# 64x64 TensorE tiles, half-partition loads on two queues and an early half-width start in a gated-attention + bilinear-FFN kernel

## The chip, the cores and the metric

One core of a Trainium2 chip runs the whole program. The metric is the device time of one execution in microseconds (us), less is better. Engines: TensorE (PE; PEld is its weight load), VectorE (DVE), ScalarE (ACT), GpSimd (POOL), and SyncE (SP), which only issues DMAs.

## The reference, cut to what matters

```python
# q, k, v, alpha: (B=4, H=8, S=768, D=48); per batch and head
state = alpha[t][:, None] * state + outer(k[t], v[t])
y[t]  = q[t] @ state
# x = y as (3072, 384); weights 384x1536, 384x1536, 1536x384
out = ((x @ w_a) * (x @ w_b)) @ w_out
```

## The kernel before

The sequence is cut into six chunks of 128 positions, and a chunk holds all four batches. The 64 partitions of a half g hold 64 position pairs of two batches; the position within a pair is the index r, a free index. The batch within a half is u.

For a chunk the attention runs through these stages: `load` (alpha, v, k, q; each tile in two DMAs of 64 partitions with rows of 384 bytes), `logs` (Ln on ACT, pair sums), `stA` (cumulative sums by a float32 matmul, then four Exp on ACT), `mul` (scaled Q and K, on POOL after the first chunk), `vcast` and `vshift` (V to bf16, then four DMAs move it to natural position order, `vb`), `decay`, `stC` (eight transposes, copied out as `qk`), `stD` (scores, times the causal mask, `m`), `stY` (output from the state `Sb` and from `vb`, copied to `xT`), `fill` (six small DMAs that complete `xT`: heads have 48 rows and lie in 64), and `stK` (state update).

The FFN of a chunk is 12 pairs `ff_a(f)`, `ff_b(f)` of three matmuls of 512 columns, and 4 `ff_o(m)` of 12 matmuls of 384 columns. The FFN of chunk c and the attention of chunks c+1 and c+2 are interleaved by hand: the tables `PLAN` and `STEADY` give the slot behind which each stage is written, a slot being one f (0 to 11) or one m (12 to 15). Every engine takes its instructions in the written order.

PSUM: tag `f` has four banks for the FFN (and for the first chunk's stages), `t1` and `t2` one each for `stC` and for `stA`/`stY`, `s2` two for `stD`/`stK`. At the start SP issues all loads of chunk 0 one after the other; POOL then issues 16 loads of w_a and w_b with a cast to bf16, three of w_out, and two memsets by which chunk 1's alpha and k loads are held back until then.

Of the kernel before, what the change touches and what calls it, by code (L numbers as in the profile page):

```python
# [11 lines left out]
ALU = mybir.AluOpType  # L12


@with_exitstack
def kernel(
# [14 lines left out]
    C = 128  # L31
# [50 lines left out]
    vz = cst.tile([C, B, KT, 2, DP], BF16, name="vz")  # L82
    nc.vector.memset(vz, 0.0)
# [24 lines left out]
    chunks = [Chunk(c) for c in range(NCH)]  # L108

# [4 lines left out]
    def load(ch, what, us):  # L114
# [53 lines left out]
    def decay(ch):  # L168
# [7 lines left out]
        for r in range(2):  # L176
            nc.sync.dma_start(out=ch.bl[r * DP:r * DP + D].rearrange("d b a -> d (b a)"),
                              in_=row[:, :, r, :].rearrange("g a d -> d (g a)"), allow_slow_non_contiguous=True)

    def stC(ch, u, h, tag="t1", act=False):  # L180
        i = ch.c % 2
        t = bank(tag, 4 if tag == "f" else 1, BF16, [C, 2, 2, 2, 2, HC])
        for p in range(2):
            for j, src in enumerate((Qp[i], Kp[i])):
# [5 lines left out]
        if act:  # L190
# [4 lines left out]
    def stD(ch, u, h, tags=None):  # L195
        qk = ch.qk[u, h]
        ch.m[u, h] = m = wk.tile([C, 2, 4, C], BF16, name="m", bufs=4)
        if tags is None:
            s2 = bank("s2", 1, F32, [C, 2, 4, C])
            sc = [s2[:, 0], s2[:, 1]]  # L200
        else:
            sc = [bank(t, 1, F32, [C, 4, C]) for t in tags]
        for p in range(2):
            for g in range(2):
                for r in range(2):
                    rs = slice(r * DP, (r + 1) * DP)
                    nc.tensor.matmul(sc[r][:, 2 * p + g, :], lhsT=qk[rs, 1, p, g, :], rhs=qk[rs, 0, p, g, :], start=True, stop=True)  # L207
        if tags is None:
            nc.vector.tensor_mul(m.rearrange("p r a s -> p (r a) s"), s2.rearrange("p r a s -> p (r a) s"), maskn(8))  # L209
        else:  # L210
            for r in range(2):
                nc.vector.tensor_mul(m[:, r], sc[r], maskn(4))

    def alloc_x(ch):

        ch.xT = wk.tile([128, KT + 1, B, C], BF16, name="xT")

    def evac(ch, u, ts, y, act=True, gaps=True):

        n = ts.stop - ts.start  # L220
        o_ = ch.xT[:, ts, u::2, :].rearrange("p t g (s r) -> p (t g) r s", r=2)
        i_ = y[:, :2 * n].rearrange("p a (r s) -> p a r s", r=2)
        for r in range(1 if gaps else 2):
            rs = slice(0, C) if gaps else slice(r * DP, r * DP + D)
            if act and r == 0:
                nc.scalar.activation(out=o_[rs], in_=i_[rs], func=AF.Copy)  # L226
            else:
                nc.vector.tensor_copy(o_[rs], i_[rs])  # L228

    def stY(ch, u, h):  # L230
        if not hasattr(ch, "xT"):
            alloc_x(ch)
        y = bank("t2", 1, F32, [C, 4, C])

        for p in range(2):
            for g in range(2):
                nc.tensor.matmul(y[:, 2 * p + g, :], lhsT=Sb[:, 2 * g + u, 2 * h + p, :], rhs=ch.qk[u, h][:, 0, p, g, :],  # L237
                                 start=(p == 0 and g == 0), stop=False, skip_group_check=True)
        for p in range(2):
            for g in range(2):  # L240
                for r in range(2):
                    hd = 2 * (2 * h + p) + r
                    nc.tensor.matmul(y[r * DP:r * DP + D, 2 * p + g, :], lhsT=ch.vb[:, 2 * g + u, hd * D:(hd + 1) * D], rhs=ch.m[u, h][:, r, 2 * p + g, :],  # L243
                                     start=False, stop=True, skip_group_check=True)
        evac(ch, u, slice(2 * h, 2 * h + 2), y, gaps=(ch.c > 1 or h == 1))

    def stYz(ch, u, tags, act):

        if u == 0:
            alloc_x(ch)  # L250
        for h, n in ((1, 1), (0, 2)):
            y = bank(tags, 4, F32, [C, 4, C])
            for p in range(n):
                for g in range(2):
                    for r in range(2):
                        nc.tensor.matmul(y[r * DP:(r + 1) * DP, 2 * p + g, :], lhsT=vz[:, 2 * g + u, 2 * h + p, r, :], rhs=ch.m[u, 1][:, r, 2 + g, :],
                                         start=(p == 0 and g == 0), stop=False, skip_group_check=True)
            for p in range(n):
                for g in range(2):
                    for r in range(2):  # L260
                        hd = 2 * (2 * h + p) + r
                        nc.tensor.matmul(y[r * DP:r * DP + D, 2 * p + g, :], lhsT=ch.vb[:, 2 * g + u, hd * D:(hd + 1) * D], rhs=ch.m[u, h][:, r, 2 * p + g, :],
                                         start=False, stop=True, skip_group_check=True)
            evac(ch, u, slice(2 * h, 2 * h + n), y, act=(h == 0))

    def fill(ch):
        for t in range(KT):
            for r in range(2):
                eng = nc.sync if ch.c > 1 else (nc.gpsimd, nc.scalar)[r]
                eng.dma_start(out=ch.xT[r * DP + D:(r + 1) * DP, t], in_=ch.xT[r * DP + t * G:r * DP + (t + 1) * G, KT])  # L270

    def stK(ch, u):
# [4 lines left out]
        for p in range(P2):  # L277
            for r in range(2):
                for g in range(2):
                    gs = slice(g * HC, (g + 1) * HC)  # L280
                    nc.tensor.matmul(kv[:, g, p * 2 * D:(p + 1) * 2 * D], lhsT=Kp[i][gs, u, r, 2 * p:2 * p + 2, :].rearrange("s h d -> s (h d)"),  # L281
                                     rhs=ch.vx[gs, r, u, 2 * p:2 * p + 2, :].rearrange("s h d -> s (h d)"), start=(r == 0), stop=(r == 1))
        tmp = None if ch.c == 0 else wk.tile([C, 2, P2, D], F32, name="tmp")
        for r in range(2):
            rs = slice(r * DP, r * DP + D)
            x = kv[rs, :, :P2 * 2 * D].rearrange("p g (a e) -> p g a e", a=P2)[:, :, :, r * D:(r + 1) * D]
            so = Sb[rs, u::2, :, r * DP:r * DP + D]
            bl = ch.bl[rs, u::2, :].rearrange("p g (a o) -> p g a o", o=1).broadcast_to([D, 2, P2, D])
# [183 lines left out]
```

## Time and profile before

| | |
|---|---|
| median of 3 runs | 245.22 us (244.45 to 245.22) |
| the profiled execution | 244.67 us |
| its span, first to last instruction | 242.8 us |
| PE busy | 202.2 us, 83% of the span |
| granted PE clock, mean | 0.93 |
| DMA | 30.31 MB, mean 125 GB/s |

A busy PE is an average over stages with different limits; the rows below cut the span by chunks. 1.9 us of the profiled execution lie outside the span.

### The profile page before, as it was taken

The page shows a single profiled execution, that of the slowest core. Times are in us where ns is not written, and L with a number is a line of the kernel's source. Part 1 is how long each engine was busy: PE and PEld are TensorE (multiplying, and loading weights), DVE is VectorE, ACT ScalarE, POOL GpSimd, SP SyncE. Part 2 cuts the span into 40 slices and gives each one's busy share as a digit, 9 for nine tenths or more (in the row PEclk, how much of TensorE's full clock was granted, in tenths as well). Part 3 has the DMA queues.
Part 4 walks back from the last instruction along what each step waited for, and adds up shares of the span by engine and source line. Part 5 has one row for each costly group of instructions (what it writes and reads, how often), then busy time and mean ns, then how long its engine had stood idle before and what let it go on. Part 6 is the DMA issues. An engine that isn't in the chain of part 4 may idle for free.

```text
span 242.8 us, 4155 instructions
## 1 busy us (share of the span) xinstructions
PE 202.2 (83%) x1556; PEld 109.9 (45%) x1576; DVE 126.4 (52%) x180; ACT 121.6 (50%) x194; POOL 73.0 (30%) x79
## 2 busy tenths in 40 slices
PE   0426699399862978998999999999998999999994
PEld 0124544135641333565455554555454555554452
DVE  3266737055234456862577932978625886215510
ACT  2545223574732674484654386544758445334421
POOL 3028610046020549032680235902238400000000
PEclk9985579859996599999999999999999999999999
DMA  7999999993996802999239992239992300120002
GB/s 125 190 205 201 162 179 204 215 208 73 160 173 132 203 19 51 176 204 221 68 69 180 191 153 80 68 71 197 191 146 100 97 3 0 49 99 3 0 32 97
DMA packets 67915, 30.31 MB, mean 125 GB/s; under 512 B 59716, under 2 KB 67128, under 8 KB 67896
## 3 DMA queue, kind: packets, MB, share of 16 engines
q1 hardware_dynamic: 64328, 26.42, 61.8%
q0 software_dynamic: 3472, 3.59, 9.7%
q8 instruction: 12, 0.20, 0.4%
q10 hardware_dynamic: 96, 0.05, 0.1%
q14 instruction: 7, 0.06, 0.1%
HBM read 25.98 MB, written 4.75 MB: 127 GB/s over the span
## 4 chain that ended last, share of the span: by engine, by line
PE 59%; DMA 14%; ACT 6%; issue 6%; POOL 6%; SPq 4%; DVE 2%; POOLq 0%; ACTq 0%; DVEq 0%
PE f L304 16%; PE f L311 16%; PE f L317 14%; DMA a_t<-in_alpha_dram 7%; SPq L118 4%; PE t L187 4%; PE s L207 3%; POOL Qp L166 3%; DMA k_t<-in_k_dram 3%; PE t L243 3%; DMA wa_t<-in_moe_w_a_dram 2%; PE t L158 2%; ACT la L137 2%; PE s L281 2%; PE t L237 2%
## 5 line engine op out<-in xcount | busy, mean ns | idle before, releaser
L304 PE MATMUL f<-xT,wa_t 128*128 128x512 bf16 x214 | 61.5, 395 | 7.1 <-ACT as__495 L306 3.9
L311 PE MATMUL f<-xT,wb_t 128*128 128x512 bf16 x198 | 58.6, 392 | 1.4 <-issue 0.6
L317 PE MATMUL f<-wo_t,prod 128*128 128x384 bf16 x288 | 49.7, 326 | 0.7 <-DVE prod L312 0.7
L317 PEld LDWEIGHTS <-prod 128*128 128x128 bf16 x288 | 27.8, 98 | 21.5 <-DVE prod L312 1.7
L304 PEld LDWEIGHTS <-wa_t 128*128 128x128 bf16 x216 | 21.7, 101 | 34.5 <-issue 9.3
L209 DVE TENSOR_TENSOR m<-s,mask 128x1024 bf16<-128x1024 f32 x22 | 26.9, 1224 | 17.3 <-PE s L207 17.3
L311 PEld LDWEIGHTS <-wb_t 128*128 128x128 bf16 x216 | 18.9, 100 | 20.7 <-issue 3.1
L293 POOL TENSOR_TENSOR Sb<-tmp,bl 48x384 bf16<-48x384 f32 x16 | 13.2, 826 | 45.4 <-DVE tmp L292 44.8
L166 POOL TENSOR_TENSOR Kp<-k_t,invb 128x768 bf16<-128x768 f32 x10 | 18.7, 1873 | 20.4 <-ACT invb L162 14.9
L319 ACT ACTIVATE ot<-f 128x384 f32<-128x384 f32 x24 | 11.8, 491 | 25.6 <-PE f L317 25.6
L226 ACT ACTIVATE xT<-t 128x512 bf16<-128x512 f32 (+1 forms) x20 | 14.9, 743 | 6.2 <-PE t L243 3.2
L166 POOL TENSOR_TENSOR Qp<-q_t,beta 128x768 bf16<-128x768 f32 x9 | 17.1, 1900 | 0.0
L159 DVE TENSOR_TENSOR le<-t,la 128x384 f32<-128x384 f32 x10 | 5.6, 558 | 20.2 <-PE t L158 20.2
L139 POOL TENSOR_TENSOR l<-la 128x768 f32<-128x768 f32 x5 | 9.1, 1812 | 21.7 <-ACT la L137 21.5
L187 PEld LDWEIGHTS <-Qp 128*128 128x128 bf16 x96 | 8.4, 105 | 13.6 <-DVE Qp L166 7.2
L193 DVE COPY qk<-t 128x1024 bf16<-128x1024 bf16 x16 | 11.1, 692 | 2.6 <-PE t L187 2.2
L158 PE MATMUL t<-l,ut_f 128*128 128x384 f32 x20 | 9.4, 555 | 3.4 <-ACT beta L161 2.5
L292 DVE TENSOR_TENSOR tmp<-s,Sb 48x384 f32<-48x384 f32 x16 | 8.9, 554 | 6.2 <-PE s L281 5.9
L137 ACT ACTIVATE la<-a_t 128x1536 f32<-128x1536 f32 (+1 forms) x7 | 9.0, 1298 | 5.4 <-DMA a_t<-in_alpha_dram 5.4
L237 PE MATMUL t<-qk,Sb 128*128 128x128 bf16 x80 | 7.9, 223 | 4.1 <-DVE xT L228 3.3
L187 PE MATMUL t<-ident,Qp 128*128 128x128 bf16 x76 | 9.5, 220 | 1.5 <-POOL Qp L166 1.5
L158 PE MATMUL f<-l,ut_f 128*128 128x384 f32 x4 | 2.9, 880 | 9.2 <-DVE l L139 9.2
(213 smaller groups left out, 269.6 us busy)
## 6 DMA issues: line engine op xcount, KB each, us to landing
a_t<-in_alpha_dram SPq DMA_DIRECT2D x12, 384.0 KB
v_t<-in_v_dram SPq DMA_DIRECT2D x12, 384.0 KB
k_t<-in_k_dram SPq DMA_DIRECT2D x24, 192.0 KB
q_t<-in_q_dram SPq DMA_DIRECT2D x24, 192.0 KB
out_dram<-ot SPq DMA_DIRECT2D x24, 192.0 KB
vb<-vx SPq DMA_DIRECT2D x24, 96.0 KB
wo_t<-in_moe_w_out_dram POOLq DMA_DIRECT2D x3, 384.0 KB, 12.6
wa_t<-in_moe_w_a_dram POOLq DMA_DIRECT2D x2, 288.0 KB, 6.6
```

What stands on the lines that cost most here:

```text
L137: nc.scalar.activation(out=ch.la[:, us].rearrange("p b h r d -> p (b h r d)"), in_=ch.a[:, us].rearrange("p b h r d -> p (b h r d)"), func ...
L158: nc.tensor.matmul(p, lhsT=ut_f32, rhs=ch.l2[:, u].rearrange("p h d -> p (h d)"), start=True, stop=True)
L166: eng.tensor_mul(dst[ch.c % 2][:, u, :, :, :D], src[:, u].rearrange("p h r d -> p r h d"), by[:, u])
L187: nc.tensor.transpose(t[:, j, p, :, r, :], src[:, u, r, hp:hp + 2, :].rearrange("s h d -> s (h d)"), ident)
L209: nc.vector.tensor_mul(m.rearrange("p r a s -> p (r a) s"), s2.rearrange("p r a s -> p (r a) s"), maskn(8))
L226: nc.scalar.activation(out=o_[rs], in_=i_[rs], func=AF.Copy)
L237: nc.tensor.matmul(y[:, 2 * p + g, :], lhsT=Sb[:, 2 * g + u, 2 * h + p, :], rhs=ch.qk[u, h][:, 0, p, g, :], start=(p == 0 and g == 0), sto ...
L293: nc.gpsimd.tensor_mul(so, tmp[rs], bl)
L304: nc.tensor.matmul(ap, lhsT=wa_t[:, kk, f * 128:(f + 1) * 128], rhs=ff_x(ch)[:, kk, :], start=(kk == 0), stop=(kk == KT - 1))
L311: nc.tensor.matmul(bp, lhsT=wb_t[:, kk, f * 128:(f + 1) * 128], rhs=ff_x(ch)[:, kk, :], start=(kk == 0), stop=(kk == KT - 1))
L317: nc.tensor.matmul(op, lhsT=ch.prod[:, f, m * C:(m + 1) * C], rhs=wo_t[:, f, :], start=(f == 0), stop=(f == NFF - 1))
L319: nc.scalar.activation(out=ot, in_=op, func=AF.Copy)
```

## The change

Stages are now written from two tables: `START` for all that stands ahead of the first chunk's FFN, and `PLAN[c]` with steps of one half slot (0 to 23 for ff_a and ff_b, 24 to 27 for ff_o). The parts:

- Chunk 0's loads go half by half to two queues: partitions 0 to 63 by SP, 64 to 127 by ACT or POOL; batch half u=0 of alpha, k and q is first. Chunk 1's loads are split between SP and POOL, between the weight loads on POOL. Later chunks load by SP alone.
- w_a and w_b come in columns 0:256, 256:768, 768:1536 (24 DMAs).
- Matmuls on constants (`warm`) are written between the first stages.
- `ff_a`, `ff_b` of f = 0, 1, 2 of chunk 0 run once for each half of the columns (u=0, u=1).
- V is not shifted: `vshift` and `vb` go, `stD` computes scores by position parity rk in 64x64 tiles (16 matmuls in place of 8), `stY` is one stage for a u (8 with `Sb`, 32 with `vx`, in place of 2 x (4 + 8)), `stK` has 32 matmuls of 48 columns in place of 16 of 96. Outputs stay in parity order, and each `ff_o` is stored by two DMAs.
- Chunk 1's `fill` is done by six matmuls with a selection matrix `gap`.
- `stA` and `stC` use the four `f` banks; `stY` has two banks of its own (`y2`).

```diff
+START = [
+    (0, "ld a 0 YS"), (0, "ld a 1 YS"), (0, "ld k 0 YS"), (0, "ld q 0 YS"),
+    (0, "warm 40"), (0, "vz0"), (0, "L 0 V"), (0, "L 1 V"), (0, "exp"),
+    (0, "ld k 1 YP"), (0, "ld q 1 YP"), (0, "ld v * YP"), (0, "S0 P"),
+    (0, "A 0"), (0, "warm 8"), (0, "A 1"), (0, "warm 8"), (0, "dec"),
...
+    (0, "ff 0 0"), (0, "ff 1 0"), (0, "Y 1 S dma"), (0, "ff 2 0"), (0, "ff 0 1"), (0, "ff 1 1"), (0, "ff 2 1"),
+]
...
-            nc.sync.dma_start(out=t[g * HC:(g + 1) * HC, us].rearrange("p b h r d -> p (b h) (r d)"),
+            engs[g].dma_start(out=t[g * HC:(g + 1) * HC, us].rearrange("p b h r d -> p (b h) (r d)"),
...
-                    nc.tensor.matmul(sc[r][:, 2 * p + g, :], lhsT=qk[rs, 1, p, g, :], rhs=qk[rs, 0, p, g, :], start=True, stop=True)
+                        nc.tensor.matmul(s2[g * HC:(g + 1) * HC, r, p, rk, :], lhsT=qk[rs, 1, p, g, rk * HC:(rk + 1) * HC], rhs=qk[rs, 0, p, g, :], start=True, stop=True)
...
+        for p in reversed(range(P2 if ch.c > 0 else KT)):
+            for rk in range(2):
                 for g in range(2):
                     for r in range(2):
+                        mm(g, r, p, D, ch.vx[g * HC:(g + 1) * HC, u, 2 * p + r, rk, :], ch.m[u, p // 2][g * HC:(g + 1) * HC, r, p % 2, rk, :])
...
-                    nc.tensor.matmul(kv[:, g, p * 2 * D:(p + 1) * 2 * D], lhsT=Kp[i][gs, u, r, 2 * p:2 * p + 2, :].rearrange("s h d -> s (h d)"),
+                    nc.tensor.matmul(kv[r * DP:(r + 1) * DP, g, p * D:(p + 1) * D], lhsT=Kp[i][gs, u, rk, hd, :], rhs=ch.vx[gs, u, hd, rk, :], start=(rk == 0), stop=(rk == 1))
...
-        nc.sync.dma_start(out=out[m * S + ch.c * C:m * S + (ch.c + 1) * C, :], in_=ot)
+        for r in range(2):
+            nc.sync.dma_start(out=rows[r], in_=ot[r * HC:(r + 1) * HC])
```

On SP, at the program's start, stand before the change (64x16x96 is one half of a tile for both u, 64x8x96 for one u):

```order
L118 DMA a_t<-in_alpha_dram 64x16x96 x2
L118 DMA v_t<-in_v_dram 64x16x96 x2
L118 DMA k_t<-in_k_dram 64x8x96 x2
L118 DMA q_t<-in_q_dram 64x8x96 x2
L118 DMA k_t<-in_k_dram 64x8x96 x2
L118 DMA q_t<-in_q_dram 64x8x96 x2
L149 DMA vb<-vx 64x768 x4
```

and with the change:

```order
L164 DMA a_t<-in_alpha_dram 64x8x96 x2
L164 DMA k_t<-in_k_dram 64x8x96
L164 DMA q_t<-in_q_dram 64x8x96
L164 DMA k_t<-in_k_dram 64x8x96
L164 DMA q_t<-in_q_dram 64x8x96
L164 DMA v_t<-in_v_dram 64x16x96
L216 DMA row<-beta 2x1x384 x2
```

SP issues one half only; the other half's first four loads moved to ACT, its last three to POOL. V moved from second place to last.

On ACT, at the end of chunk 0's FFN, where chunk 1's attention ends (qk, ot and xT are the copies of `stC`, `ff_o` and `stY`; as_ is `ff_a` of chunk 1), stand before the change:

```order
L226 ACTIVATE xT<-t_684 128x4x2x64
L191 ACTIVATE qk<-t_709 128x1024
L319 ACTIVATE ot<-f 128x384
L226 ACTIVATE xT<-t_747 128x4x2x64
L270 DMA xT<-xT 16x512 x3
L226 ACTIVATE xT<-t_767 48x4x2x64
L226 ACTIVATE xT<-t_793 48x4x2x64
L306 ACTIVATE as__813<-f 128x512
```

and with the change:

```order
L233 ACTIVATE qk<-f 128x1024
L287 ACTIVATE xT<-y_920 128x2x128
L287 ACTIVATE xT<-y_920 128x2x3x128
L233 ACTIVATE qk<-f 128x1024
L362 ACTIVATE ot<-f 128x384 x2
L287 ACTIVATE xT<-y_1052 128x2x128
L287 ACTIVATE xT<-y_1052 128x2x3x128
L345 ACTIVATE as__1106<-f 128x512
```

The u=0 half of chunk 1 is now copied out ahead of the last two `ff_o`, and no DMA stands between the copies.

## Rows read from the trace of the kernel before

**Rows 1.** The page, shares by engine and 40 slices of 6.07 us
```profile
PE 202.2 (83%) x1556; PEld 109.9 (45%) x1576; DVE 126.4 (52%) x180; ACT 121.6 (50%) x194; POOL 73.0 (30%) x79
...
DMA  7999999993996802999239992239992300120002
```

**Rows 2.** Windows by chunk of the FFN: from:to, length, busy (count) of each engine, clock, DMA share, GB/s
```profile
0.00:30.36 30.36, 12.10 (x116) 8.77 (x117) 15.94 (x29) 12.98 (x19) 13.12 (x34) 0.77 1.16 177
30.36:78.31 47.95, 36.56 (x266) 18.99 (x268) 19.97 (x27) 23.02 (x35) 9.53 (x9) 0.86 1.04 167
78.31:118.01 39.70, 35.71 (x286) 18.92 (x291) 22.34 (x33) 24.14 (x37) 15.99 (x13) 0.92 0.76 141
118.01:152.96 34.95, 33.36 (x283) 18.16 (x288) 21.62 (x31) 20.38 (x36) 16.61 (x13) 1.00 0.75 130
152.96:186.38 33.42, 31.91 (x266) 17.35 (x269) 21.36 (x29) 19.07 (x33) 12.99 (x10) 1.00 0.78 134
186.38:215.97 29.59, 29.18 (x230) 16.13 (x233) 16.87 (x21) 12.35 (x22) 4.75 (x3) 1.00 0.14 43
215.97:242.80 26.83, 23.35 (x119) 11.60 (x119) 8.26 (x12) 9.62 (x17) 0.00 (x0) 1.00 0.11 39
```

**Rows 3.** The chain that ended last, in order of time: start, length, what
```profile
27.35 17.78 DMA a_t<-in_alpha_dram
...
66.76 1.95 PE f L317 x12
...
70.52 2.75 DMA xT<-xT
...
76.11 0.64 PE t L243 x8
...
78.31 1.44 PE f L304 x3
...
86.88 0.66 PE t L158 x2
...
91.62 1.82 POOL Qp L166
...
93.49 0.62 PE t L187 x8
```

**Rows 4.** Windows of the loads, columns as in rows 2
```profile
3.00:3.50 0.50, 0.00 (x0) 0.00 (x0) 0.38 (x3) 0.00 (x0) 0.00 (x0) 1.00 1.03 287
3.50:4.00 0.50, 0.00 (x0) 0.00 (x0) 0.50 (x2) 0.00 (x0) 0.00 (x0) 1.00 1.28 280
...
5.00:7.00 2.00, 0.00 (x0) 0.00 (x0) 0.12 (x1) 0.00 (x0) 0.00 (x0) 1.00 1.35 186
...
18.00:20.00 2.00, 1.23 (x14) 0.70 (x12) 0.97 (x2) 1.75 (x2) 2.00 (x5) 0.50 1.15 244
...
54.00:56.00 2.00, 2.00 (x10) 0.82 (x10) 1.18 (x2) 1.34 (x3) 2.00 (x2) 1.00 0.99 203
56.00:58.00 2.00, 2.00 (x13) 1.15 (x12) 0.60 (x2) 1.44 (x4) 2.00 (x2) 1.00 0.32 81
```

**Rows 5.** Timeline of PE in steady chunks: start, length, instruction, count
```profile
188.44 0.81 PE L304 MATMUL f<-xT,wa_t 128*128 128x512 bf16 x3
189.19 0.40 PE L207 MATMUL s<-qk 64*128 64x128 bf16 x8
189.51 0.82 PE L311 MATMUL f<-xT,wb_t 128*128 128x512 bf16 x3
...
166.01 0.51 PE L281 MATMUL s<-vx,Kp 64*128 64x96 bf16 x16
```

**Rows 6.** Groups by line and shape: line, engine, operation, count, busy, mean ns, idle before
```profile
L209 DVE TENSOR_TENSOR m<-s,mask 128x1024 bf16<-128x1024 f32 x22 | 26.9, 1224 | 17.3 <-PE s L207 17.3
...
L166 POOL TENSOR_TENSOR Kp<-k_t,invb 128x768 bf16<-128x768 f32 x10 | 18.7, 1873 | 20.4 <-ACT invb L162 14.9
...
L193 DVE COPY qk<-t 128x1024 bf16<-128x1024 bf16 x16 | 11.1, 692 | 2.6 <-PE t L187 2.2
...
L312 DVE TENSOR_TENSOR prod<-as__370,f 128x512 bf16<-128x512 bf16 x1 | 0.7, 687 | 3.0 <-PE f L311 3.0
```

More of the change, by code (lines that the diff above doesn't have):

```diff
@@ L193, in stC, with stD @@
             nc.vector.tensor_copy(o_, i_)
[L195 removed]
+    def stD(ch, u, h, tag="s2"):
         qk = ch.qk[u, h]
[L197 to L202, printed above, removed]
[L203 to L212 removed]
@@ L214, in alloc_x @@
[L214 to L245, printed above, removed]
@@ new lines, in evac @@
+        def evac(lo, hi):
+            o_, i_ = ch.xT[:, lo:hi, u::2, :].rearrange("p a g s -> p g a s"), y[:, :, lo:hi, :]
+            if eng is nc.vector:
+                nc.vector.tensor_copy(o_, i_)
+            else:
+                nc.scalar.activation(out=o_, in_=i_, func=AF.Copy)
+        if ch.c > 0 and how == "pe":
+            evac(KT, P2)
+            for t in range(KT):
+                for g in range(2):
+                    nc.tensor.matmul(y[:, g, t, :], lhsT=gap[:, t].rearrange("p r d -> p (r d)"), rhs=ch.xT[:, KT, 2 * g + u, :], start=False, stop=True, skip_group_check=True)
+            evac(0, KT)
+        else:
+            evac(0, P2 if ch.c > 0 else KT)
@@ new lines, with us, table, gate_w @@
+    HALVES = (slice(0, B, 2), slice(1, B, 2))
+    def us(u):
+        return ALL if u == "*" else ONE[int(u)]
+    def table(func):
+        nc.scalar.activation(out=junk, in_=one, func=func)
+    def gate_w(x, what):
+        nc.gpsimd.tensor_copy(go, getattr(x, what)[0:1, 1, 0, 0, 0:1])
+    def gate_in(x, what):
+        nc.gpsimd.memset(getattr(x, what)[0:1, 0, 0, 0, 0:1], 0.0)
+    def zero_vz():
+        nc.vector.memset(vz, 0.0)
+    def zero_s(e):
+        ENG[e].memset(Sb, 0.0)
+    def make_vz(x):
+        for r in range(2):
+            nc.vector.tensor_copy(vz[:, :, :, :, r, D:].rearrange("p u k t g -> p u (k t) g"), x.v[:, :, 6 + r].rearrange("p u k (t g) -> p u (k t) g", g=G))
@@ L408, with do @@
+    def do(chunk, stage):
+        st = stage.split()
+        STAGES[st[0]](chunks[chunk], *st[1:])
+    done = {(0, int(stage.split()[1])) for _, stage in START if stage.startswith("ff")}
+    done |= {(chunk, int(stage.split()[1])) for c in range(NCH) for _, chunk, stage in PLAN[c] if stage.startswith("ff")}
+    for chunk, stage in START:
+        do(chunk, stage)
     for c in range(NCH):
         ch = chunks[c]
-        nx = chunks[c + 1] if c + 1 < NCH else None
-        n2 = chunks[c + 2] if c + 2 < NCH else None
@@ L435 @@
-        for f in range(NFF):
-            ff_a(ch, f)
-            run(h, f)
-            ff_b(ch, f)
-        for m in range(B):
-            ff_o(ch, m)
-            run(h, NFF + m)
+        for i in range(2 * NFF + B):
+            if i >= 2 * NFF:
+                ff_o(ch, i - 2 * NFF)
+            elif (c, i // 2) not in done:
+                (ff_b if i % 2 else ff_a)(ch, i // 2)
+            for step, chunk, stage in PLAN[c]:
+                if step == i:
+                    do(chunk, stage)
```

309 lines of the change are left out of this document (144 added, 165 removed), and 4 rows, old and new, of the table START.

## The prediction

> **What bounds the kernel now.** I read the page first: PE is busy for 83% of the span, and the DMA row is full up to the tenth slice [rows 1]. A mean says little here, so I cut the span at the starts of the chunks' FFNs [rows 2]. From 118 us on PE is busy for 118 of 125 us at the full clock: PE's own work bounds that part. Ahead of it 118 us pass for two chunks, and PE is busy for 84 of them, partly at half clock (0.77, 0.86, 0.92). A steady chunk needs 30 to 35 us, so nearly all that can be won lies before 118 us.
>
> Then the chain [rows 3]. Up to 45.1 us it is DMA: chunk 1's alpha takes 17.8 us to land behind the weights. The loads in flight run at 186 to 205 GB/s and end at about 56.5 us: in the window from 56 to 58 the rate falls to 81 [rows 4]. From there to 78.3 us, 21.8 us, the chain is chunk 1's attention: the last ff_o group ends at 68.7, and after it come a copy, the `fill` DMA of 2.75 us, two more copies, a mask, the last output matmuls, two copies again. PE has next to no other work in those 9.6 us.
>
> **The parts and their prices.** The sum goes against the profiled execution, span 242.8 us plus 1.87 outside it, 244.67; the median of the three runs, 245.22, is 0.2% above.
>
> *Loads by halves.* A chunk's four tensors are 3.15 MB (4 x 4 x 8 x 128 x 48 x 4 bytes). The first half tile, alone on its queue, ran at 287 and 280 GB/s; then the rate fell to 186 and stayed near there while halves followed one another on one queue [rows 4]. So a rate near 283 is possible with these 384-byte rows, and what holds it down afterwards sets in only when a transfer has gone on for a while. I read this as a limit on the side of the 64 partitions written, filled after 1 to 2 us; then two halves in flight together have twice the sink. When weights and loads overlap, 18 to 20 us, it is 244. Bounds: 195 GB/s as now (16.2 us for chunk 0) and 283 (11.1 us). I take 283 where both halves are in flight, which the first row is nearest to: -5 us for chunk 0, and -1.5 for chunk 1, whose SP halves start beside the weights and whose POOL halves meet them only in part. Chunk 1's data is complete at about 50 us in place of 56.5.
>
> The Trainium skill, DMA: Bandwidth & Descriptors, section Rules for kernel authors, speaks against this: two transfers to disjoint partition halves share the same 16 engines and serialize, so it advises against the split. By that rule the term would be 0; the trace's first microsecond at 287 neither confirms nor refutes it, since only one half was in flight. The Trainium skill's SBUF — State Buffer, section on Door 1, says on the other hand that partitions 0 to 63 reach 8 of 16 ports and measured 196 GB/s for them against 328 for 128 partitions; the 186 to 205 here agree.
>
> *Chunk 1's attention.* With the change, after the last q: k and q products on POOL end about 3 us later (1.87 each, the first overlapped [rows 6]); then eight transposes 0.45, Y of u=0 about 1.9 with its first copy, scores 0.33, transposes 0.45, an ff_o 1.95 [rows 3], scores 0.33, an ff_o 1.95, Y of u=1 with matmul fill and two copies 3.0: 13.4 us. So FFN 1 starts at 50 + 13.4 = 63.4 in place of 78.3: **-14.9 us** with the loads. The earlier start of chunk 0's FFN (about 22 us in place of 30.4: 5 from the loads, some 3 from beginning on half of the columns) I cost at nothing beyond that: its later part waits for the third set of weights and for chunk 1's alpha, so the DMA chain covers it. If that cover went, it would be worth up to 8 us.
>
> *FFN 1.* Its stretch is 39.7 us at clock 0.92 [rows 2], so 0.08 x 2 x 39.7 = 6 us at half clock and 3 us lost. With ff_o directly ahead of it and gaps of 2 to 3 us I expect full clock: **-3 us**. Its other stall stays: from chunk 2's stA at 86.9 to the transposes at 93.5, since Kp and Qp on POOL come between [rows 3]; the tables leave the same distance.
>
> *The tiles.* Twelve ff_o matmuls of 384 columns take 1.95 us [rows 3], 0.423 ns a column: 54 ns for 128 columns, 217 for 512. Eight score matmuls, one by one, would need 0.43 us; from their start to the next FFN matmul there are 0.32 (189.19 to 189.51), so two row tiles run at once: 4 x 0.054 = 0.22. The other 0.10, and as much ahead of the group (189.19 against 188.44 + 3 x 0.217), are the price of changing the tile shape. The state update's 16 matmuls of 96 columns would need 0.65 us one by one and show 0.51 with the last one's tail [rows 5], two at once again: 8 x 0.041 = 0.33. Nothing in the trace runs four at once. If four do, 16 score matmuls cost what 8 do, 32 V matmuls what 2 x 8 do, the state update between -0.15 and +0.15 each, and since Y's V part and the scores behind it now share one shape, a chunk has 14 shape changes for 17: -0.3 us a chunk, **-1 us**, lower bound -2.5. If only two do, scores cost +0.21 each (x4), V +0.42 (x2), the state +0.1 to +0.3 (x2): about +2 a chunk, +9 in all. I take four at once, since row pairs do overlap, and column pairs too: 8 V matmuls at half clock take 0.64 us where one by one they would need 0.86 [rows 3].
>
> *Added waits.* `stA` and `stC` now take f banks. A bank taken by stA stays with ACT until its last Exp, less than the 4.7 us from there to Qp on POOL; in the FFN slots three groups (1.95 us) pass before PE wants it again, and the rest hides in the wait for Qp that stands there anyway [rows 3]. Chunk 3's first transposes are written 4.4 us of PE work after its stA (an ff_o, a state update, an stA, an ff_a, and stA itself), where the chain to Qp takes 6.6 (86.88 to 93.49): 2.2, of which a part falls together with the FFN's own wait on ACT behind the Exps: +1.5. Bank waits elsewhere +1, the second store DMA at the end +0.5: **+3 us**. vshift, its DMAs and the unshuffled vcast free SP and DVE, which in steady chunks work beside PE's FFN: 0; without that cover a shift would cost about what fill does, 2.75 us [rows 3].
>
> Sum: 242.8 - 14.9 - 3 - 1 + 3 = 226.9, plus 1.87: **228.5 us**, rounded.
>
> **Rivals.**
> 1. *The halves serialize.* The loads stay at 195 GB/s: +5 + 1.5 = 6.5, 235 us. For it: one set of DMA engines, busy share 1.3 throughout the loads. Against: the 287. This is also the case in which the split does not do what it says, and where the skill's rule leads.
> 2. *Only two tiles at once.* 228.5 + 9 + 1 = 238. For it: no row shows four, and the weight loads double in number. Against: in the state update two matmuls start every 41 ns, so issuing is no limit at the 54 ns that four tiles would take.
> 3. *More than forecast.* Chunk 0's FFN is through early enough that only two ff_o stand in chunk 1's chain, and FFN 1 loses its other waits: it is busy for 35.7 of 39.7 us [rows 2], so -4, and -2.5 for a shorter chain: 222.
> 4. *Slower: DVE becomes the bound.* In the first half of a steady chunk DVE does, for two f, two products, one qk copy and one mask: 2 x 0.69 + 0.69 + 1.22 = 3.29 us [rows 6] against PE's 2.6 + 0.45 + 0.33 = 3.38. Until now a late qk copy held `t1` alone; now it holds a bank of the FFN. To eat the 16 us won, each of some 24 such pairs would have to cost 0.67 us more than PE's work, so the mask would have to take 1.98 us in place of 1.22. For it: margin 0.09 us. Against: shape and size of the mask product are unchanged, and DVE is busy for 21 of 33 to 35 us in FFN 2 and 3. Past that point: above 245.
>
> **How the numbers follow.** Forecast 0.5 (its own range 223 to 233, for the clock at the start and the chain's length), rival 1 0.2, rival 2 0.12, rival 3 0.1, rival 4 0.06; 0.02 remain for no change. 0.3% of 245 us is 0.7 us, about what this kernel's measurement can tell; all cases but the last two lie below by more: faster 0.92, same 0.02, slower 0.06. The range takes in the forecast, rival 1 and most of rivals 2 and 3: 219 to 238.
>
> **What would show it.** Loads: windows of 3 to 14 us at 260 GB/s or more (rival 1: about 200), chunk 0's data in by 14 us, chunk 1's by 50. Chain: first matmul of FFN 1 near 63 us, no gap above 3 us ahead of it, clock 1.00 afterwards. Tiles: 16 score matmuls in about 0.4 us from first start to last end (two at once: 0.6). Waits: the stretch of FFN 2 at about 35 us, FFN 3 at 33, FFN 4 at 29. The prediction fails if chunk 1's alpha still lands at 45 us because SP's halves slow the weights, if PE falls back to half clock in chunk 0's FFN for more than a few us, or if rows of PE in steady chunks show waits for DVE at the f banks.

## The result, and the profile after

The change takes 4.6% off: 233.48 us median against 245.22; the ratio of the means is 0.954, 95% interval 0.948 to 0.960. Executions more than 1.5% above the fastest of their kernel, two of them of 407 us, are left out of all ratios here. The forecast was 228.5 us in a range of 219 to 238, so sign and range hold and the middle is 5 us too low. The profiled execution took 233.83 us, span 232.1.

From the page after the change, to be held against [rows 1] (shares by engine; DMA share in 40 slices of 5.8 us):

```profile
PE 205.6 (89%) x2238; PEld 116.2 (50%) x2238; DVE 119.6 (52%) x174; ACT 120.1 (52%) x192; POOL 86.3 (37%) x96
...
DMA  6999999995999319992399811699723000230023
```

PE is busy no less than before (205.6 us, 202.2 before); it waits less. The windows cut at the starts of the chunks' FFNs show where (from:to, length, busy time of each engine, clock, DMA share, GB/s):

```profile
23.54:70.69 47.15, 37.54 (x442) 21.86 (x442) 19.29 (x29) 23.89 (x39) 20.11 (x25) 0.93 1.10 180
70.69:107.75 37.06, 34.59 (x432) 18.42 (x432) 23.14 (x33) 23.59 (x36) 16.55 (x13) 1.00 0.86 144
107.75:143.34 35.59, 33.32 (x364) 17.92 (x365) 20.34 (x29) 19.45 (x33) 17.75 (x14) 0.95 0.69 111
143.34:175.29 31.95, 31.37 (x366) 17.33 (x364) 19.68 (x27) 18.13 (x29) 12.93 (x10) 1.00 0.79 129
175.29:204.23 28.94, 28.94 (x298) 16.11 (x296) 15.55 (x20) 11.18 (x18) 3.03 (x2) 1.00 0.14 33
204.23:232.10 27.87, 23.51 (x122) 11.65 (x119) 8.26 (x12) 9.62 (x17) 0.00 (x0) 0.96 0.18 42
```

Against [rows 2]: FFN 1 starts at 70.7 in place of 78.3 (-7.6, forecast -14.9). FFN 1 takes 37.1 in place of 39.7 us, at clock 1.00. FFN 2 takes 35.6 for 35.0 (with FFN 1 together 72.7 for 74.7). FFN 3 takes 31.95 for 33.4, FFN 4 28.9 for 29.6. The whole miss lies in the start of FFN 1.

The chain that ended last, up to there (start, length, what):

```profile
4.19 9.77 DMA k_t<-in_k_dram
...
44.23 11.84 DMA v_t<-in_v_dram
...
57.70 0.35 PE y L247 x16
58.05 2.07 PE f L360 x12
```

Two things are seen. The 16 score matmuls take 0.35 us (eight took 0.32 before). Two at once would have needed 8 x 0.054 = 0.43 us for the columns alone, and in the trace their starts come in groups of four: four 64x64 tiles run at once. And loads lead the chain up to 56.1 us, when DVE takes the second half of chunk 1's v; before, they led it up to 45.1.

Chunk 1's loads did not end earlier than before. DMA's rate falls to 60 GB/s at 54.5 us and to 5 at 55. Before, the traffic up to 56.5 us [rows 4], which the prediction took for loads, ends with the four moves of `vb` (96 KB each, issued from 53.15 us on behind the loads): SP's queue moved 0.64 MB from 53 to 57 us, and 0.39 of it were these. At 207 GB/s the remaining 0.25 MB put the end of the loads at about 54.2 us, an estimate.

The windows of the loads, to be held against [rows 4]:

```profile
3.00:5.00 2.00, 2.00 (x23) 2.00 (x21) 0.49 (x2) 0.00 (x0) 1.63 (x6) 1.00 1.21 244
5.00:7.00 2.00, 0.43 (x8) 0.25 (x5) 1.96 (x8) 0.84 (x1) 2.00 (x4) 1.00 1.30 220
7.00:9.00 2.00, 0.04 (x1) 0.07 (x1) 1.83 (x6) 1.58 (x2) 1.72 (x1) 0.82 1.30 237
...
11.00:13.00 2.00, 2.00 (x11) 1.21 (x9) 0.32 (x2) 1.69 (x4) 0.00 (x0) 0.50 1.07 205
13.00:15.00 2.00, 1.28 (x11) 0.75 (x8) 2.00 (x3) 1.56 (x4) 0.98 (x3) 0.50 1.08 186
...
19.00:21.00 2.00, 1.67 (x47) 1.14 (x44) 2.00 (x2) 1.61 (x2) 1.25 (x3) 1.00 0.79 63
21.00:23.00 2.00, 1.30 (x64) 1.06 (x64) 1.69 (x4) 2.00 (x4) 2.00 (x4) 1.00 1.21 119
```

Two halves on two hardware queues (SP's and ACT's) run at 220 to 237 GB/s, not at the 283 that the sum used. The high rate belongs to the first microsecond, with two halves in flight as with one: in half microseconds from 3 us on it is 299, 271 and 189 here, where it was 287, 280 and 175. From 11 us, with POOL's halves in flight, the gain is gone. The view of the queues says why. First 4 to 9 us (SP is q1, ACT q10), then 10 to 14 us (POOL is q0): packets, MB, share of 16 engines.

```profile
q1 hardware_dynamic: 1535, 0.57, 65.5%
q10 hardware_dynamic: 1464, 0.55, 62.9%
```
```profile
q0 software_dynamic: 210, 0.74, 91.3%
q1 hardware_dynamic: 291, 0.11, 19.0%
```

SP and ACT share evenly, in packets of one row of 384 bytes. Beside POOL, whose packets hold 3.5 KB on average (0.74 MB in 210), SP's half gets 0.11 MB against 0.74: its tile is complete only when the starved half is. The Trainium skill, DMA: Bandwidth & Descriptors, section Queues, rings and completion order, states that each DMA engine takes turns between queues by whole packets; these counts agree.

### The profile page after: what moved, and what is told of

It is laid out like the page before. It is cut to its first block, busy times and chain, and to the rows that moved or that the text cites. A ratio compares the mean times of both kernels' runs of the same rounds, so it can differ in the third digit from the quotient of the medians.

```text
span 232.1 us, 5488 instructions
## 1 busy us (share of the span) xinstructions
PE 205.6 (89%) x2238; PEld 116.2 (50%) x2238; DVE 119.6 (52%) x174; ACT 120.1 (52%) x192; POOL 86.3 (37%) x96
## 3 DMA queue, kind: packets, MB, share of 16 engines
q1 hardware_dynamic: 54440, 20.91, 54.5%
## 4 chain that ended last, share of the span: by engine, by line
PE 60%; DMA 16%; SPq 8%; ACT 5%; issue 4%; POOL 4%; DVE 1%; ACTq 0%; POOLq 0%; DVEq 0%
PE f L360 19%; PE f L351 15%; PE f L343 14%; SPq L164 6%; DMA v_t<-in_v_dram 5%; DMA k_t<-in_k_dram 4%; PE f L229 3%; PE s L247 3%; DMA wb_t<-in_moe_w_b_dram 2%; DMA wa_t<-in_moe_w_a_dram 2%; PE y L260 2%; PE y L266 2%; PE f L200 2%; DMA a_t<-in_alpha_dram 1%; ACT la L178 1%
## 5 line engine op out<-in xcount | busy, mean ns | idle before, releaser
L351 PE MATMUL f<-xT,wb_t 128*128 128x512 bf16 (+1 forms) x225 | 61.5, 384 | 2.8 <-DMA wb_t<-in_moe_w_b_dram 2.8
L343 PE MATMUL f<-xT,wa_t 128*128 128x512 bf16 (+1 forms) x225 | 60.6, 378 | 3.4 <-DMA xT<-xT 2.0
L360 PEld LDWEIGHTS <-prod 128*128 128x128 bf16 x288 | 27.8, 98 | 21.8 <-issue 2.9
L248 DVE TENSOR_TENSOR m<-s,mask 128x1024 bf16<-128x1024 f32 x22 | 26.9, 1223 | 15.7 <-PE s L247 15.7
L351 PEld LDWEIGHTS <-wb_t 128*128 128x128 bf16 x225 | 19.9, 101 | 21.5 <-issue 5.0
L200 PE MATMUL f<-l,ut_f 128*128 128x384 f32 x24 | 12.8, 619 | 7.5 <-DVE l L180 6.9
L235 DVE COPY qk<-f 128x1024 bf16<-128x1024 bf16 x16 | 11.1, 692 | 14.0 <-PE f L229 13.9
L287 ACT ACTIVATE xT<-y 128x1024 bf16<-128x1024 f32 (+2 forms) x14 | 12.2, 872 | 6.0 <-PE y L260 4.8
L201 DVE TENSOR_TENSOR le<-f,la 128x384 f32<-128x384 f32 x12 | 6.7, 557 | 15.8 <-PE f L200 15.6
L229 PE MATMUL f<-ident,Qp 128*128 128x128 bf16 x96 | 10.0, 230 | 2.4 <-POOL Qp L208 2.1
L247 PEld LDWEIGHTS <-qk 64*64 64x64 bf16 x384 | 6.6, 109 | 8.1 <-issue 3.1
L229 PE MATMUL f<-ident,Kp 128*128 128x128 bf16 x96 | 9.8, 227 | 0.7 <-DVE Kp L208 0.7
L247 PE MATMUL s<-qk 64*64 64x128 bf16 x352 | 9.3, 225 | 0.9 <-ACT qk L233 0.7
```

Of the source, the lines that this page charges most:

```text
L229: nc.tensor.transpose(t[:, j, p, :, r, :], src[:, u, r, hp:hp + 2, :].rearrange("s h d -> s (h d)"), ident)
L247: nc.tensor.matmul(s2[g * HC:(g + 1) * HC, r, p, rk, :], lhsT=qk[rs, 1, p, g, rk * HC:(rk + 1) * HC], rhs=qk[rs, 0, p, g, :], start=True, ...
L248: nc.vector.tensor_mul(m.rearrange("p r a k s -> p (r a) (k s)"), s2.rearrange("p r a k s -> p (r a) (k s)"), maskn(4))
L287: nc.scalar.activation(out=o_, in_=i_, func=AF.Copy)
L343: nc.tensor.matmul(ap, lhsT=wa_t[:, kk, f * 128:(f + 1) * 128], rhs=ff_x(ch, us)[:, kk], start=(kk == 0), stop=(kk == KT - 1))
L351: nc.tensor.matmul(bp, lhsT=wb_t[:, kk, f * 128:(f + 1) * 128], rhs=ff_x(ch, us)[:, kk], start=(kk == 0), stop=(kk == KT - 1))
```

## The experiments

All are edits of the changed kernel, timed against the kernel before on their chip; none leaves out part of the computation. Runs that did not run side by side are compared by these ratios; for the changed kernel the first was 0.954. Its repetition stands first, as the yardstick.

**The changed kernel again**, no edit.

> The changed kernel itself, beside the versions below, on the same chip and against the same runs of the kernel before. Expected: ratio 0.950 to 0.956, FFN 1's first matmul at 70 to 71.5 us, last half of v at 55 to 57 us. Another start of FFN 1 by 1 us or more would say that single profiles of the experiments can't tell 1 us.

Measured: 233.85 us, ratio 0.9562 (0.952 to 0.960). FFN 1 began at 72.5 us, 1.8 later than in the first profile, and yet the last matmul ended as it did there (227.8 us), since FFN 1 took 36.6 us in place of 37.1 and FFN 2 34.3 in place of 35.6. So a single profile places FFN 1's start to about 2 us, and what follows can absorb that.

**Chunk 0's loads on one queue.**
```diff
-    (0, "ld a 0 YS"), (0, "ld a 1 YS"), (0, "ld k 0 YS"), (0, "ld q 0 YS"),
+    (0, "ld a 0 YY"), (0, "ld a 1 YY"), (0, "ld k 0 YY"), (0, "ld q 0 YY"),
...
-    (0, "ld k 1 YP"), (0, "ld q 1 YP"), (0, "ld v * YP"), (0, "S0 P"),
+    (0, "ld k 1 YY"), (0, "ld q 1 YY"), (0, "ld v * YY"), (0, "S0 P"),
```

> All of chunk 0's loads go through SP alone, both halves one behind the other; nothing else differs from the changed kernel (233.5 us). Theory A (the two hardware queues together move little more than one: 209 to 234 GB/s in the stretches from 4 to 12 us after the change, 186 to 205 on one queue before it): stretches of 3 to 12 us at 190 to 210 GB/s, the matmul that chunk 0's first half-width FFN stage begins with 0 to 1.5 us later than 23.6 us, FFN 1 at 70 to 72 us, time 232.5 to 235. Theory B, the prediction's (two queues in parallel carry 283 GB/s, and POOL's halves spoil it later): stretches at 150 GB/s or less and 3 us or more lost, 236.5 or above. Theory C (POOL's queue takes the share that SP's half needed: 180 against 29 GB/s from 10 to 14 us): with no half of chunk 0 on POOL the last half of k is in before 13 us, and the time falls by 1 to 2 us in spite of one queue.

Measured: 231.78 us, ratio 0.947 (0.943 to 0.952). Its profile is of an execution of 407 us; the rates of one queue are read from a later version, below. Theory B, the prediction's, falls for this version: without the split nothing is lost, and perhaps 1 to 2 us are won, as theory C has it.

**Only the later loads of chunk 0 taken off POOL** (the second pair of lines above, the first as changed).

> Chunk 0's first loads stay split over SP and ACT; the later ones (second half of k and q, all of v) that had one half on POOL now have both on SP. Theory A (POOL's packets of eleven rows each take the share of SP's packets of one row, so that SP's half of k, on which the gate of the weight loads waits, comes in at 13.96 us): that half lands at 11 to 12.5 us, the gate opens 1.5 to 3 us earlier, the weights follow by as much, FFN 1 begins 1 to 2 us earlier than 70.78, time 231.5 to 232.5. Theory B (the sixteen DMA engines are full at that time whatever queue feeds them, and the weights that follow are bound by their own eight outstanding transfers): the gate earlier, weights in at 34 us as before, FFN 1 within 0.7 us of 70.78, time 233 to 234.

Measured: 232.39 us, ratio 0.949 (0.944 to 0.954). From the chain of waits:

```profile
4.25 7.36 DMA k_t<-in_k_dram
...
11.66 0.17 POOL go L382
```

The second half of k lands at 11.6 us in place of 13.96: that POOL's packets hold SP's half back is shown. But FFN 1 starts at 70.1, 0.6 earlier, as theory B has it and within what a profile can place. The time is in theory A's range, but its interval overlaps the unedited kernel's. Of the 2.4 us by which the gate (POOL's `go`, behind which the weight loads stand) opens earlier, nothing that can be told from none arrives at FFN 1.

**Weights in 16 DMAs** in place of 24.
```diff
-    ... (0, "W 0 256"), (0, "W 256 768"), (0, "W 768 1536"), ...
+    ... (0, "W 0 512"), (0, "W 512 1536"), ...
```

> The weights wa and wb in two parts of 512 and 1024 columns (16 DMAs) as before the change, in place of three of 256, 512 and 768 (24 DMAs); all else as changed. Theory A (24 DMAs with eight outstanding make the stretch of 18 to 30 us slow: 79 to 159 GB/s): these stretches at 150 GB/s or more, last part of wb in 2 to 3 us before 34 us, chunk 1's alpha 2 us before 42, FFN 1 1 to 2 us earlier, time 231.5 to 232.5. Theory B (the engines are busy all the while with short rows, whatever the cut): weights in within 1 us of 34, FFN 1 within 0.7 us of 70.78, and the first half-width stage later by 2 to 4 us since its weights come in a larger part; time 233 to 234.5.

Measured: 231.4 us, ratio 0.945 (0.941 to 0.950). The windows that answer to 63 and 119 GB/s above:

```profile
19.00:21.00 2.00, 1.48 (x43) 0.96 (x40) 2.00 (x3) 1.80 (x3) 1.19 (x3) 1.00 1.17 172
21.00:23.00 2.00, 1.45 (x64) 1.16 (x65) 1.48 (x5) 2.00 (x3) 1.32 (x3) 1.00 1.15 158
```

Cut into three sets, the weights come at a lower rate just where they are wanted. FFN 1 starts at 68.8 here, 1.9 us before the first profile of the changed kernel and 3.7 before the second: theory A, though wb's last part still lands only at 34.3 us.

**Chunk 1's loads on one queue** (in the same line, all of chunk 1's `YP` become `YY`).

> Chunk 1's loads go through SP alone, both halves one behind the other, in place of SP and POOL; all else as changed (233.5 us, FFN 1's first matmul at 70.7). Theory A (the rate of the sixteen engines sets when the data are in, however they are split: about 220 GB/s from 34 to 50 us): last half of v lands at 54 to 56.5 us, FFN 1 at 70 to 71.5, time 233 to 234.5. Theory B, the prediction's (halves on two queues bring chunk 1's data in earlier): without the split the last data come 3 us later or more, 236 us or above. Theory C (POOL's queue takes the share of SP's halves, and each transfer is in only when SP's half is): without POOL's halves the data come in 1 to 3 us earlier, 231 to 232.5, unless alpha now comes behind Wo's transfers: then PE waits longer than 3.35 us for chunk 1's first cumulative product, and nothing is gained.

Measured: 235.92 us, ratio 0.966 (0.959 to 0.973), FFN 1 at 73.5. This version parts chunk 1's last data from its alpha. Windows, and then PE's and ACT's timeline:

```profile
53.00:55.00 2.00, 2.00 (x10) 0.84 (x9) 1.25 (x2) 1.30 (x4) 2.00 (x2) 0.87 0.89 153
55.00:57.00 2.00, 1.39 (x12) 0.67 (x11) 1.08 (x2) 1.85 (x4) 2.00 (x2) 1.00 0.03 8
```
```profile
45.04 1.28 ACT L178 ACT_TABLE_LOAD   x1 [5.43 <-DMA a_t<-in_alpha_dram]
46.33 1.48 ACT L178 ACTIVATE la<-a_t 128x1536 f32<-128x1536 f32 x1
48.86 1.65 PE L200 MATMUL f<-l,ut_f 128*128 128x384 f32 x2 [8.59 <-DVE l L180]
```

The data ends by 55 us, no later than with the split, and yet FFN 1 starts 2.8 us later than in the first profile: it is alpha, landing at 45 us in place of 42, for which ACT, DVE and PE wait, PE for 8.6 us. It is theory C's exception. By the times the split of chunk 1's loads is worth about 2.5 us, and not as the prediction had it. That alpha makes all of this is not shown: in the repetition alpha landed at 44.3 us with the split, and FFN 1 started only 1.0 us before this version's.

**Chunk 2's fill by matmuls.**
```diff
-(20, 2, "Y 0 S dma"), ... (26, 2, "Y 1 S dma"), (26, 2, "fill YY"),
+(20, 2, "Y 0 S pe"), ... (26, 2, "Y 1 S pe"),
```

> Chunk 2's V-product output is completed by the matmuls that fill the gap rows (as chunk 1's) in place of the six fill DMAs; all else as changed. Theory A (chunk 2's FFN begins late because its fill DMAs stand on SP's queue behind two store DMAs for each output: FFN 2's first matmul at 107.85 us waits on, ff_a's tile 0 for the fill until 110.15, and the clock is at half from 110.8 to 114.2): no wait there above 0.7 us, FFN 2 at 33.0 to 34.0 us in place of 35.6, clock full throughout, time 231 to 232. Theory B (the prediction's added waits are elsewhere: bank waits of the 64x64 tiles with ff's tiles): the wait for the fill goes but another of about 2 us follows, FFN 2 at 35 to 36, time 233 to 234.

Measured: 235.7 us, ratio 0.964 (0.960 to 0.969): slower. The timeline of PE at FFN 2's start, first of the changed kernel, then of this one (L229 are the transposes of the scaled K and Q, `Kp` and `Qp`):

```profile
107.75 0.38 PE L343 MATMUL f<-xT,wa_t 128*128 128x512 bf16 x1 [0.34 <-DMA xT<-xT]
108.94 0.39 PE L343 MATMUL f<-xT,wa_t 128*128 128x512 bf16 x1 [0.81 <-DMA xT<-xT]
110.20 0.39 PE L343 MATMUL f<-xT,wa_t 128*128 128x512 bf16 x1 [0.87 <-DMA xT<-xT]
```
```profile
111.11 0.40 PE L229 MATMUL f<-ident,Kp 128*128 128x128 bf16 x4 [0.56 <-POOL Kp L208]
112.88 0.40 PE L229 MATMUL f<-ident,Qp 128*128 128x128 bf16 x4 [1.37 <-POOL Qp L208]
```

The wait for the fill (2.0 us in three parts) goes, and one of as much for POOL's Kp and Qp of chunk 3 stands behind it (theory B's form, at a place of the prediction's: "Chunk 3's first transposes are written 4.4 us of PE work after its stA"). The matmuls and the copies that they wait for add to FFN 1: 38.5 us.

**Both waits of FFN 2 moved.**
```diff
-(26, 2, "Y 1 S dma"), (26, 2, "fill YY"), ... (22, 3, "L * P"), (26, 3, "A 0"), ... (27, 3, "A 1"),
+(25, 2, "Y 1 S dma"), (25, 2, "fill YY"), ... (20, 3, "L * P"), (24, 3, "A 0"), ... (25, 3, "A 1"),
```

> In chunk 1's FFN only positions differ from the changed kernel: chunk 2's second V-product output and its fill DMAs one step earlier (25 in place of 26), and chunk 3's logarithm, cumulative products, exponentials and scalings two steps (one for the second product) earlier. Theory A (FFN 2's start of 107.85 us waits twice at the same place, for the fill until 110.2 and behind it for POOL's Kp and Qp until 110.4, so that taking away the fill alone, as measured, only shows the second wait of 1.4 us, and both must go): neither wait above 0.5 us, FFN 2 at 33.0 to 34.2 us in place of 35.6, clock full from 110 to 115 us, total 231 to 232.3. Theory B (the positions push the waits to another place: banks of f, or ACT's table switches before the output copies): FFN 1 longer than 37.1 by 1 us or more, total 233 to 235.

Measured: 232.42 us, ratio 0.951 (0.945 to 0.956). FFN 1 and FFN 2 as windows:

```profile
71.23:108.89 37.66, 34.20 (x428) 18.48 (x432) 23.58 (x32) 24.93 (x40) 21.65 (x16) 1.00 0.83 137
108.89:141.67 32.78, 30.96 (x368) 17.31 (x365) 20.68 (x29) 17.78 (x29) 11.95 (x11) 1.00 0.79 126
```

FFN 2 gets 2.8 us shorter and FFN 1 0.6 longer: theory A for the mechanism, though a wait of 0.65 us for the fill is left. Together they take 70.4 us, where the changed kernel took 72.7 in its first profile and 70.9 in its second. In the second the granted clock stayed at 1.00 there; in the first it fell to 0.50, the lower of its two levels, from 110.8 to 114.2 us, right behind the three waits above. So the gain is 0.4 us against the one and 2.2 against the other; the interval overlaps the unedited kernel's.

**No start on half of the rows** (the six `ff` steps at the end of START taken out).

> Chunk 0's FFN is not begun on half of the rows: its first three column blocks run at full width once both halves of its V product are there, as all the others do; all else as changed. Theory A, the prediction's (the start is hidden: what chunk 1's chain waits for is its data): first FFN matmul at 27 to 31 us in place of 23.6, last of chunk 0's FFN and FFN 1's start within 0.7 us of 70.7, time 233 to 234. Theory B (PE's rows stand in a fixed order, and the stages of chunk 1 stand behind more of chunk 0's FFN): chunk 1's first cumulative product at 47 us or later in place of 45.9, FFN 1 1 to 3 us later, 234.5 to 236.5.

Measured: 234.23 us, ratio 0.958 (0.954 to 0.963): within the noise of the changed kernel. In the profile the FFN began at 25.6 and FFN 1 at 73.6, but ACT's logarithm of alpha began at 42.9, as early as with the half start, and PE waited 4.5 us for it: up to there the early start is covered, as predicted. What made FFN 1 late came behind it: DVE's cast of the last v half took 1.88 us beside POOL's Qp where in the first profile it took 0.56, PE waited 2.4 us for the product behind it, and the clock fell (mean 0.72 from 58 to 64 us). Whether that belongs to this edit one profile can't say.

**No warming matmuls** (all five `warm` steps taken out).

> Without the matmuls on constants that keep PE busy in the first 20 us; all else as changed. Theory A, the prediction's (they are worth nothing, what follows waits for loads): time within 0.7 us of 233.5, though the granted clock of the stretches from 5 to 30 us differs. Theory B (they bring the clock up for chunk 0's scores and first FFN stages, or, the other way, they take the clock down early: 0.50 from 8.4 to 18.6 us stands right behind 3.4 us of them): chunk 0's first FFN matmul 1 us or more away from 23.6 and FFN 1's start 1 us or more away from 70.7, up or down.

Measured: 232.82 us, ratio 0.950 (0.945 to 0.956), FFN 1 at 69.75. The clock, from 5 to 16 and from 16 to 21.5 us, of the changed kernel:

```profile
5.00:16.00 11.00, 6.55 (x40) 4.29 (x38) 7.50 (x16) 6.72 (x13) 5.69 (x9) 0.65 1.22 214
16.00:21.50 5.50, 4.74 (x88) 3.92 (x85) 3.62 (x7) 4.01 (x5) 4.48 (x9) 0.77 1.17 125
```

and of this one:

```profile
5.00:16.00 11.00, 4.38 (x32) 2.32 (x36) 7.46 (x15) 7.77 (x14) 6.15 (x9) 0.97 1.22 215
16.00:21.50 5.50, 5.22 (x121) 3.98 (x117) 4.85 (x6) 4.01 (x5) 5.24 (x10) 0.50 1.16 128
```

With them the half clock comes from 8.4 us on, without them from about 15, and FFN 1's start moves by less than a profile can place: they are worth nothing, and if anything a loss of 1 us that these runs can't tell from none. That they bring the half clock is not shown either: in the version with the later loads off POOL, which has them all, the clock stays at 1.00 up to 27 us.

**Weights in 16 DMAs and both waits moved.**

> Two edits together that each took time away: the weights in 16 DMAs, and chunk 2's fill and chunk 3's preparation earlier. If they act at different places (the one on FFN 1's start, the other on FFN 2's), the gains add: FFN 1's start at 68.5 to 70, FFN 2 at 33 us, time 3.5 to 4.5 us below the changed kernel, 229 to 230. If both only shift the same wait: 1 to 2.5 us below it.

Measured: 232.1 us (229.7 to 234.8), ratio 0.947 (0.941 to 0.952), 1.75 us by medians below the changed kernel beside it, the intervals just touching. FFN 1 and 2 together again take 70.45 us. The expected 3.5 to 4.5 don't come: in the profiled run (234.3 us) the last part of wb landed only at 36.2 us and FFN 1 started at 73.4, so the earlier start that the 16 DMAs brought above is not there in each execution.

**The same, and chunk 0 on one queue.**

> As the version with both edits, and all of chunk 0's loads on SP alone. By the prediction's term (two queues carry 283 GB/s where one carries 200) chunk 0's first FFN matmul comes 3 us later and the time rises by 2 us or more; by the reading after (two carry 210 to 234, one 186 to 205 before, and POOL's halves starve SP's) stretches of 3 to 12 us at 185 to 215 GB/s, second half of k in at 12.5 to 14 us, no matmul of FFN 1 later by over 1 us, time within 1 us of the version with both edits.

Measured: 236.72 us (231.0 to 239.3; too spread for a ratio). The rates of one queue:

```profile
5.00:7.00 2.00, 0.42 (x8) 0.24 (x5) 1.90 (x4) 0.84 (x1) 1.13 (x1) 1.00 1.27 203
7.00:9.00 2.00, 0.00 (x0) 0.00 (x0) 1.86 (x8) 1.39 (x2) 0.00 (x0) 0.81 1.32 204
...
11.00:13.00 2.00, 2.00 (x11) 1.21 (x9) 0.54 (x1) 1.43 (x4) 0.61 (x2) 0.50 1.32 203
```

203 and 204 against 220 and 237: the split is worth 8 to 16% of the rate while only SP and ACT feed the engines, and next to nothing from 11 to 13 us (203 against 205). The time is 4.6 us above the version before, as much as the prediction's term would ask, but not where it puts it: the first FFN matmul came at 23.9 us, 0.4 later than in the changed kernel and 1.7 later than in the version before, not 3. What the chain of waits names is chunk 0's state update, behind a 3 KB transfer of 4-byte elements (`bl`) that SP issued at 21.8 us. The chain of waits, and the queues from 22 to 38 us:

```profile
21.82 15.99 DMA bl<-row
37.84 0.57 DVE Sb L323
```
```profile
q0 software_dynamic: 1491, 2.43, 98.3%
q1 hardware_dynamic: 2249, 0.27, 26.6%
```

SP's queue moves 0.27 MB in 16 us beside POOL's 2.43. It looks like the same starvation at another place, but no run shows it: with 16 weight DMAs alone the queues carried much the same (0.41 and 2.51 MB), and `bl`, issued at 20.4 us, held nothing up. The version without the split of chunk 0 but with 24 weight DMAs, above, did not lose time; which of the edits brings the late landing was not parted.

**The same, and no warming matmuls.**

> As the version before it, and without the matmuls that keep PE busy at the start. If these are worth nothing: within 0.7 us of it. If they take the clock down early (0.50 from 8.4 to 18.6 us right behind them), chunk 0's scores and first FFN stages run at the full clock earlier and the time falls by 1 us or more; if they bring it up, it rises by as much.

Measured: 235.93 us, ratio 0.963 (0.958 to 0.969): 0.8 us below the version before it, which itself spreads over 8 us, so again no worth is seen. The state update waits for the same transfer (until 37.7 us).

## Why the prediction was right, and where it missed

Right in sign and range: what could be won lay before 118 us, and nearly all of it was won there, but from the rest of the chain and not from the loads. Step by step:

*Loads: the step that failed.* "I take 283 where both halves are in flight" and "chunk 1's data is complete at about 50 us". Two hardware queues carried 220 to 237, one 203; POOL's halves held SP's back; chunk 1's loads ended at about 55 us, no earlier than before, and DVE took the last of them at 56.1. The 56.5 us from which the 6.5 were subtracted was misread: its tail is the traffic of `vb`. That is rival 1 in its effect (235 forecast, 233.5 measured). The half microseconds at 287 and 280 were the start of a transfer, and no rate to build on; with two halves in flight it lasts no longer, so the second half does not double the sink. The rule cited from the Trainium skill (DMA: Bandwidth & Descriptors, section Rules for kernel authors), that two halves serialize, lies nearer: by it the term is 0. Measured is 8 to 16% of the rate, and without the split of chunk 0 alone nothing is lost in the time.

*The chain to FFN 1: the wrong start.* The sum let it begin at the last data. The 13.4 us from there are not far off (14.5 from the cast of v in the first profile), but something else sets the start. The table shows ACT's logarithm of chunk 1's alpha (`la`), how long ACT had waited for alpha right before it, the second cast of v, and FFN 1's first matmul, all in us:

| kernel | `la` starts | wait for alpha | second cast of v starts | FFN 1 starts | `la` to FFN 1 |
|---|---|---|---|---|---|
| 16 weight DMAs | 42.3 | none | 53.7 | 68.8 | 26.5 |
| later loads off POOL | 42.8 | 0.8 | 54.3 | 70.1 | 27.3 |
| no warming | 42.8 | 2.9 | 54.8 | 69.8 | 26.9 |
| no half start | 42.9 | 1.3 | 56.1 | 73.6 | 30.7 |
| fill by matmuls | 43.1 | none | 55.3 | 71.2 | 28.2 |
| changed | 43.4 | 0.2 | 56.2 | 70.7 | 27.3 |
| both waits moved | 45.1 | none | 55.9 | 71.2 | 26.1 |
| changed, again | 45.6 | 3.0 | 56.1 | 72.5 | 26.9 |
| 16 DMAs, both waits | 46.2 | none | 56.4 | 73.4 | 27.2 |
| chunk 1 on one queue | 46.3 | 5.4 | 56.5 | 73.5 | 27.2 |
| 16 DMAs, both waits, one queue, no warming | 46.8 | none | 57.0 | 73.9 | 27.2 |
| 16 DMAs, both waits, one queue | 47.3 | none | 57.5 | 74.6 | 27.3 |

Over 5 us of shift FFN 1 starts 26.1 to 27.3 us behind `la`; the version without the half start is the exception told above, and fill by matmuls has 28.2. Before the change it was 31.8 (46.5 to 78.3). So in the first profile the 7.6 us won are 3.1 from `la` and 4.5 from the shorter chain behind it. What shortened it (shift, `fill` and shuffled copies gone, u=0 copied out early) no run parts. In the first profile the chain names v, but the wait that puts it there is 0.3 us long, for the last product of chunk 0, which DVE makes behind the cast of v. PE's and ACT's timeline there:

```profile
57.37 0.34 PE L360 MATMUL f<-wo_t,prod 128*128 128x384 bf16 x1 [0.27 <-DVE prod L353]
...
42.10 1.28 ACT L178 ACT_TABLE_LOAD   x1 [0.19 <-DMA a_t<-in_alpha_dram]
```

By the table, data at 50 us alone would have won next to nothing; this was not tried.

What sets `la` itself differs from version to version. With alpha later, as in the repetition, ACT waits for it. Where ACT does not wait for alpha, it comes to `la` late because its copies for chunk 0's FFN stand ahead in the written order, and these waited for weights or for the state update. With 16 weight DMAs the chain of waits runs from wb:

```profile
25.04 9.27 DMA wb_t<-in_moe_w_b_dram
34.55 0.81 PE f L351 x3
...
41.02 1.28 ACT L178
42.31 1.49 ACT la L178
```

The prediction named both, the third set of weights and chunk 1's alpha, as what covers an early start, and put neither into the sum. Whichever comes last, alpha or that part of chunk 0's FFN, starts the 27 us, so to bring only the one forward would not help in every version. Alpha first, ahead of the last weights, was not tried.

*FFN 1:* -3 forecast; the stretch lost 2.6, at clock 1.00 as said. *The tiles:* four at once, as taken, and rival 2 is refuted. Where the clock is full before and after, FFN 3 lost 1.5 us and FFN 4 0.65. PE's busy time fell by 0.54 and 0.24 of that, near the -0.3 a chunk of the forecast; the rest are short waits that went, and no run parts them. *Added waits:* +3 forecast. At FFN 2's start they stand where they were put (POOL's Qp), behind one that I had missed: six fill DMAs on SP's queue behind two store DMAs for each output, in place of one. The price is 0.4 to 2.2 us. The second store at the end is +1.0 for +0.5 (the last stretch is 27.87 us for 26.83; the difference lies behind the last matmul). *Half start:* 0, as said. The warming matmuls have no term in the sum; no worth of theirs is seen. *Rival 4:* among PE's waits from 68 to 148 us none of 0.5 us or more is for DVE. One sign of failure came in part: chunk 0's FFN has the half clock for 6.6 us (0.93 over 47.15 us), half as long as before (0.86 over 47.95).

The sum with what was measured: 242.8 - 7.6 - 2.6 (FFN 1) + 0.6 (FFN 2) - 1.5 (FFN 3) - 0.65 (FFN 4) + 1.0 (end) = 232.05, span 232.1. Of the span's miss of 5.2 us (226.9 forecast) the start of FFN 1 makes 7.3; the rest, forecast at -1 and measured at -3.1, gave 2.1 back. That these 2.1 us bring the number nearer to the forecast is luck: they have nothing to do with the loads. (226.9 and 1.87 make 228.8, which the forecast put at 228.5.)

The lowest of all is the changed kernel with 16 weight DMAs (231.4 us, 0.945, interval 0.941 to 0.950): below both kernels, against the changed one by about 1%.

## What to carry to other kernels

A rate seen in the first microsecond of a load said nothing here of what two queues carry; the counts of packets and bytes by queue did. Where one queue sent packets of 3.5 KB and another single rows of 384 bytes, the rows came late, and whatever needed both halves waited for them. Where a chain has two inputs that end close together, the profile names only the later one: before costing a gain, compute the end by each input alone (here `la` + 27 us beside the last data + 14.5), and ask what starts each. Before calling traffic a load, look which DMAs it is made of. And a wait taken away pays only up to the next one at the same place.

## What the hardware showed unexpectedly

Four 64x64 tiles ran at once: 16 score matmuls of 128 columns in 0.35 us. A 3 KB transfer of 4-byte elements took 16.0 us to land beside POOL's weights. And one kernel's FFN 1 start moved by 1.8 us between two executions of the same length: alpha landed 2.2 us later in the second, and a fall of the clock to 0.50 for 3.4 us, behind three waits of under 0.9 us each, came only in the first.
